# Three chained layers on one Trainium2 core: the first feed-forward gets half products and sums in DRAM, and one planner orders the whole program

## Chip, core and metric

The kernel runs on one core of a Trainium2 chip. The metric is device microseconds of one execution. TensorE (PE in the rows) multiplies matrices, VectorE (DVE) and ScalarE (ACT) work elementwise, GpSimd (POOL) and SyncE (SP) here mainly issue transfers.

## The reference

Linear attention without softmax, an RMS norm per head, then two feed-forwards over 2304 tokens of 512 features:

```python
kv  = einsum('bhsd,bhse->bhde', k, v)        # 4 batches, 8 heads, 576 tokens, head size 64
out = einsum('bhsd,bhde->bhse', q, kv)
x   = out / sqrt(mean(out**2, -1) + 1e-6) * g_norm          # then (2304, 512)
xn  = x / sqrt(mean(x**2, -1) + 1e-6) * rms_g
x   = (silu(xn @ w_gate) * (xn @ w_val)) @ w_out            # d_ff = 1536
h   = x @ w_in2
y   = where(h > 0, h, exp(min(h, 0)) - 1) @ w_out2          # d_ff = 2048
```

The weights come as 64-bit floats.

## The kernel before

**Tiling.** Features stand on partitions, tokens in columns. The 18 token tiles form five blocks: block 0 of 256 columns, blocks 1 to 4 of 512. A slice f is 128 columns of d_ff: 12 in the first feed-forward (phase 0), 16 in the second (phase 1). Every product in float32 is made of three matmuls on halves: high x high, high x low, low x high (lines 364 to 366). ScalarE rounds to the high half, VectorE subtracts to get the low one (`ah` and `al`, `xh` and `xl`). The four chunks of 128 features are c = 0 to 3.

**Weights.** `load` brings a tile of 512 KB on SP's queue into a staging buffer (`st`, `sx`: four). `convert` turns the 64-bit floats into a float32 and its halves in nine steps, seven on VectorE, one on ScalarE, one more on VectorE (lines 324 to 357).

**Phase 0.** For each f and block: gate product `pg`, value product `pv` (4 chunks x 3 matmuls each), `silu` on ScalarE, product on VectorE, halves, and then four output chunks `pb`. f = 0 and 1 stand alone (`LONE`), while attention still runs; from f = 2 on two f make a group whose output products share a bank. VectorE adds each into `acc` on chip (line 422). After the last group it is split into the new x.

**Phase 1.** Two f form a group. For the pairs of blocks (1, 2) and (3, 4), `hidden_pair` makes the four products of two f and two blocks from seven half products (Winograd's form of Strassen's scheme): sums of weights S1 to S4, sums of x T1 to T4, and ScalarE copies of partial results (`u`). Pair (3, 4) is still plain in the first two groups. Output chunks go through a buffer `part` to DRAM: the first group is written (SP), the others are added by accumulating transfers that GpSimd issues (line 618), and the last one is fetched back and added (`sofar`, line 610).

**Order.** The first stage (attention, f = 0 and 1, weights up to f = 3) is laid out by the class `Plan`: every step has an engine, a length in us, a rank and what it comes after, and the step that can start first is emitted next. What follows is written in order, with the framework's own scheduler.

Of the kernel before, what the change touches and what calls it, by code (L numbers as in the profile page):

```python
# [21 lines left out]
INF_FIELD = 2.0**-96 * 1.875  # L22


class Plan:
# [4 lines left out]
    LAG = {"DVE": (0.11, 0.13), "ACT": (0.15, 0.17), "POOL": (0.05, 0.1), "PE": (0.0, 0.15), "DMA": (0.0, 0.1)}  # L30

    def __init__(self):
        self.steps, self.ends, self.clock, self.lasts = {}, {}, {}, {}

    def add(self, name, engine, length, rank, call, after, tag=None):
        self.steps[name] = dict(
            engine=engine, length=length, rank=rank, call=call, after=list(after), tag=tag
        )
        self.clock.setdefault(engine, 0.0)

    def frees(self, tag, taker, users):

        self.lasts[tag, taker] = users

    def start(self, name, taken, bufs):
        s = self.steps[name]
        at = self.clock[s["engine"]]
        after = list(s["after"])
        if s["tag"] and len(taken[s["tag"]]) >= bufs[s["tag"]]:
            after += self.lasts.get((s["tag"], taken[s["tag"]][-bufs[s["tag"]]]), [None])  # L50
        for x in after:
            if x not in self.ends:
                return None
            engine = self.steps[x]["engine"]
            at = max(at, self.ends[x] + self.LAG[engine][engine != s["engine"]])
        return at

    def run(self, bufs):
        taken = {tag: [] for tag in bufs}
        left = {}  # L60
        for name, s in self.steps.items():
            left.setdefault(s["engine"], []).append(name)
        while any(left.values()):
            best = None
            for names in left.values():
                for name in names:
                    at = self.start(name, taken, bufs)
                    if at is not None:
                        key = at, self.steps[name]["rank"]
                        if best is None or key < best[0]:  # L70
                            best = key, name
            if best is None:
                raise ValueError(f"no step can start: {[n[:4] for n in left.values()]}")
            (at, _), name = best
            s = self.steps[name]
            left[s["engine"]].remove(name)
            if s["tag"]:
                taken[s["tag"]].append(name)
            self.clock[s["engine"]] = self.ends[name] = at + s["length"]
            s["call"]()  # L80
# [3 lines left out]
def linear_attention__swiglu__elu_kernel(  # L84
# [11 lines left out]
    out0: bass.AP,  # L96
    seq: int,
# [6 lines left out]
    F1, F2 = w_gate.shape[0], w_in2.shape[0]  # L104

# [7 lines left out]
    NMAX = 4 * P  # L113
    block_of = {i: (t, i - a) for t, (a, n) in enumerate(blocks) for i in range(a, a + n)}

# [3 lines left out]
    wp = ctx.enter_context(tc.tile_pool(name="wp", bufs=1))  # L119
    st = ctx.enter_context(tc.tile_pool(name="st", bufs=2))  # L120
    ap = ctx.enter_context(tc.tile_pool(name="ap", bufs=3))
    tp = ctx.enter_context(tc.tile_pool(name="tp", bufs=3))
    sp = ctx.enter_context(tc.tile_pool(name="sp", bufs=4))
    banks = ctx.enter_context(ExitStack())
    ps = banks.enter_context(tc.tile_pool(name="ps", bufs=1, space=PSUM))

    PSUM_BUFS = {"g": 3, "o": 5}

    def psum(tag, name):
        return ps.tile([P, 512], F32, tag=tag, name=name, bufs=PSUM_BUFS[tag])  # L130

    staged = ["st", "sx"]

    def stage(src, name):
        staged.append(staged.pop(0))
        t = st.tile([P, 2 * DM], src.dtype, tag=staged[-1], name=name)
        nc.sync.dma_start(out=t, in_=src)
        return t


    blank = const.tile([P, P], F32, name="blank")
    nc.vector.memset(blank, 0.0)
    idle = psum("g", "idle")
# [9 lines left out]
    junk = const.tile([P, DM + 1], mybir.dt.bfloat16, name="junk")  # L153

    Z = 6
    z_sb = [res.tile([P, DM + 1], F32, tag=f"z{j}", name=f"z{j}") for j in range(Z)]
# [7 lines left out]
    kv_blocks = [res.tile([P, KD, P], F32, tag=f"kvb{j}", name=f"kv{j}") for j in range(2)]  # L164
# [19 lines left out]

    def load_kv_tile(i):
        in_sb[i] = home(i)
        nc.sync.dma_start(out=in_sb[i], in_=kv[i].rearrange("t j e -> t (j e)"))
# [6 lines left out]
    def sum_kv(b, i):  # L194

        tiles = tiles_of_batch(b)
        if i == tiles[0]:
            kv_acc[b] = psum("g", f"kv{b}").rearrange("p (a e) -> p a e", a=KD)
# [17 lines left out]
    def load_q(j):  # L216
        src = q[j].rearrange("d j a t -> d (j a t)")
        if f"q{j}" in homes:
            q_sb[j] = home(f"q{j}")
            nc.sync.dma_start(out=q_sb[j], in_=src)  # L220
        else:
            q_sb[j] = stage(src, f"q{j}")
# [60 lines left out]
    def new_x(t):  # L283
        n = blocks[t][1] * P
        xh[t] = res.tile([P, KD, n], F32R, tag=f"xh{t}", name=f"xh{t}")
        xl[t] = res.tile([P, KD, n], F32R, tag=f"xl{t}", name=f"xl{t}")

    def turn(p, half):

        pt = pt_t[p, half] = psum("o", f"pt{p}_{half}").rearrange("p (c n) -> p c n", c=2)  # L290
# [18 lines left out]
    raw_sb, ready = {}, {}  # L309

    def load(src, kind, name, bufs):
        raw_sb[name] = stage(src.bitcast(U32), "r" + name)

    def convert(src, kind, name, bufs):
# [3 lines left out]
        def begin():  # L318
            raw = raw_sb.pop(name).rearrange("p (n w) -> p n w", w=2)
            t["low"], t["high"] = raw[:, :, 0], raw[:, :, 1]  # L320
            t["c"] = tp.tile([P, DM], U32, tag="tA", name="c" + name)


            nc.vector.tensor_scalar(t["c"], t["high"], 0x7FFFFFFF, None, op0=ALU.bitwise_and)
# [8 lines left out]
        def sign():  # L333
            t["w"] = tp.tile([P, DM], U32, tag="tB", name="w" + name)
# [12 lines left out]
        def add():  # L347
            wf = t["w"].bitcast(F32)
            nc.vector.tensor_tensor(wf, wf, t["c"].bitcast(F32), op=ALU.add)

        def part():
            t["h"] = wp.tile([P, DM], F32R, tag="h" + kind, name="h" + name, bufs=bufs)
            nc.scalar.activation(t["h"], t["w"].bitcast(F32), AF.Copy)

        def rest():
            l = wp.tile([P, DM], F32R, tag="l" + kind, name="l" + name, bufs=bufs)
            nc.vector.tensor_tensor(l, t["w"].bitcast(F32), t["h"].bitcast(F32), op=ALU.subtract)
            ready[name] = t["h"], l

        return [begin, scale, shift, sign, field, low, add, part, rest]  # L360

    def product(acc, w, s, xs, first, last):
        (wh, wl), (mh, ml) = w, xs
        nc.tensor.matmul(acc, wh[:, s], mh, start=first, stop=False)  # L364
        nc.tensor.matmul(acc, wh[:, s], ml, start=False, stop=False)  # L365
        nc.tensor.matmul(acc, wl[:, s], mh, start=False, stop=last)  # L366

    def into(acc, w, t):
        for c in range(KD):
            product(acc, w, slice(c * P, (c + 1) * P), (xh[t][:, c, :], xl[t][:, c, :]), c == 0, c == KD - 1)  # L370

    def act_tiles(n, name):
        h = ap.tile([P, NMAX], F32R, tag="ah", name="ah" + name, bufs=5)
        l = ap.tile([P, NMAX], F32R, tag="al", name="al" + name, bufs=5)
        return h[:, :n], l[:, :n]

    def split_act(a, n, name):
        h, l = act_tiles(n, name)
        nc.scalar.activation(h, a, AF.Copy)  # L379
        nc.vector.tensor_tensor(l, a, h.bitcast(F32), op=ALU.subtract)  # L380
        return h, l

    def gate(pg, n, name):
        s = tp.tile([P, NMAX], F32, tag="tA", name="s" + name)[:, :n]
        nc.scalar.activation(s, pg, AF.Silu)  # L385
        return s

    def gated(s, pv, n, name):
        a = tp.tile([P, NMAX], F32, tag="tB", name="a" + name)[:, :n]
        nc.vector.tensor_tensor(a, s, pv, op=ALU.mult)  # L390
        return a

    def hidden1(w, t, name):
        n = blocks[t][1] * P
        wg, wv = w
        pg = psum("g", "pg" + name)[:, :n]
        into(pg, wg, t)
        pv = psum("g", "pv" + name)[:, :n]
        into(pv, wv, t)
        return split_act(gated(gate(pg, n, name), pv, n, name), n, name)  # L400
# [581 lines left out]
```

## Time and profile before

| | |
|---|---|
| median of 3 runs | 890.13 us (889.74 to 890.29) |
| span of the profiled execution | 889.4 us |
| TensorE busy | 876.3 us |
| VectorE busy | 644.0 us |
| ScalarE busy | 409.6 us |
| GpSimd busy | 139.3 us |

The profile is of one execution; its span is the time from the first to the last instruction, and the median of the runs is 0.7 us longer. Busy times are unions of what an engine's instructions took. An engine can be busy and still be late: only where the last engine of a chain waits does it cost time.

### The profile page before, as it was taken

The page shows a single profiled execution, that of the slowest core. Times are in us where ns is not written, and L with a number is a line of the kernel's source. Part 1 is how long each engine was busy: PE and PEld are TensorE (multiplying, and loading weights), DVE is VectorE, ACT ScalarE, POOL GpSimd, SP SyncE. Part 2 cuts the span into 40 slices and gives each one's busy share as a digit, 9 for nine tenths or more (in the row PEclk, how much of TensorE's full clock was granted, in tenths as well). Part 3 has the DMA queues.
Part 4 walks back from the last instruction along what each step waited for, and adds up shares of the span by engine and source line. Part 5 has one row for each costly group of instructions (what it writes and reads, how often), then busy time and mean ns, then how long its engine had stood idle before and what let it go on. Part 6 is the DMA issues. An engine that isn't in the chain of part 4 may idle for free.

```text
span 889.4 us, 11683 instructions
## 1 busy us (share of the span) xinstructions
PE 876.3 (99%) x4324; PEld 738.8 (83%) x4324; DVE 644.0 (72%) x1229; ACT 409.6 (46%) x787; POOL 139.3 (16%) x160
## 2 busy tenths in 40 slices
PE   8999999999999999999999999999999999999998
PEld 7988888888888888888888888788888888888786
DVE  6798996567648467656867698796868677776655
ACT  2778532211212212121233577576767676666651
POOL 2465000000000000000000000033342424241400
PEclk9999999999999999999999999999999999999999
DMA  9732220102102002010200014588685949394964
GB/s 365 299 119 72 71 73 24 48 24 71 41 31 72 24 24 69 27 47 25 74 22 24 1 48 166 142 171 137 131 177 109 198 89 205 78 200 66 254 202 166
DMA packets 37145, 93.07 MB, mean 105 GB/s; under 512 B 4192, under 2 KB 4192, under 8 KB 37088
## 3 DMA queue, kind: packets, MB, share of 16 engines
q1 hardware_dynamic: 21536, 64.01, 20.4%
q0 software_dynamic: 15552, 28.32, 19.0%
q8 instruction: 34, 0.56, 0.2%
q14 instruction: 23, 0.19, 0.1%
HBM read 54.56 MB, written 37.75 MB: 104 GB/s over the span
## 4 chain that ended last, share of the span: by engine, by line
PE 69%; issue 13%; POOL 7%; DMA 5%; DVE 3%; ACT 2%; SPq 0%; POOLq 0%; ACTq 0%
PE pb L365 9%; PE pb L364 8%; PE pb L366 8%; POOL out L618 6%; PE pg L364 5%; PE pg L365 5%; PE pg L366 5%; PE pv L364 5%; PE pv L365 5%; PE pv L366 5%; PE pa L544 3%; DMA out<-part 3%; PE pc L544 2%; PE ph L364 1%; PE ph L366 1%
## 5 line engine op out<-in xcount | busy, mean ns | idle before, releaser
L618 POOL DMA_DIRECT2D out<-part x108 | 95.7, 950 | 651.7 <-ACT part L614 648.7
L379 ACT ACTIVATE ah<-a 128x512 fp32r<-128x512 f32 (+1 forms) x130 | 76.4, 590 | 157.0 <-DVE a L390 130.0
L390 DVE TENSOR_TENSOR a<-s,pv 128x512 f32<-128x512 f32 (+1 forms) x60 | 37.9, 633 | 105.4 <-PE pv L366 105.4
L380 DVE TENSOR_TENSOR al<-a,ah 128x512 fp32r<-128x512 f32 (+1 forms) x130 | 82.2, 634 | 37.7 <-ACT ah L379 37.6
L365 PE MATMUL pb<-al,hp 128*128 128x512 f32 x256 | 100.3, 392 | 0.0
L366 PE MATMUL pb<-ah,lp 128*128 128x512 f32 x256 | 99.7, 389 | 0.0
L614 ACT ACTIVATE part<-pb 128x512 f32<-128x512 f32 x126 | 73.6, 597 | 44.3 <-PE pb L366 23.3
L364 PE MATMUL pb<-ah,hp 128*128 128x512 f32 x256 | 93.0, 391 | 0.9 <-ACT part L614 0.5
L364 PE MATMUL pb<-ah,ho 128*128 128x512 f32 (+1 forms) x240 | 88.9, 370 | 0.8 <-DVE xl L304 0.4
L365 PE MATMUL pb<-al,ho 128*128 128x512 f32 (+1 forms) x240 | 88.7, 370 | 0.6 <-DVE al L784 0.6
L364 PE MATMUL pg<-xh,hg 128*128 128x512 f32 (+1 forms) x240 | 89.0, 371 | 0.0
L365 PE MATMUL pg<-xl,hg 128*128 128x512 f32 (+1 forms) x240 | 88.4, 368 | 0.0
L364 PE MATMUL pv<-xh,hv 128*128 128x512 f32 (+1 forms) x240 | 88.4, 368 | 0.0
L366 PE MATMUL pg<-xh,lg 128*128 128x512 f32 (+1 forms) x240 | 88.3, 368 | 0.0
L365 PE MATMUL pv<-xl,hv 128*128 128x512 f32 (+1 forms) x240 | 88.3, 368 | 0.0
L366 PE MATMUL pb<-ah,lo 128*128 128x512 f32 (+1 forms) x240 | 88.3, 368 | 0.0
L366 PE MATMUL pv<-xh,lv 128*128 128x512 f32 (+1 forms) x240 | 88.3, 368 | 0.0
L422 DVE TENSOR_TENSOR acc<-acc,pb 128x512 f32<-128x512 f32 (+1 forms) x120 | 74.1, 629 | 7.0 <-PE pb L366 6.3
L385 ACT ACTIVATE s<-pg 128x512 f32<-128x512 f32 (+1 forms) x60 | 33.3, 555 | 81.4 <-PE pg L366 77.9
L365 PEld LDWEIGHTS pb<-al,hp 128*128 128x128 f32 x256 | 48.1, 188 | 11.4 <-DVE al L380 1.7
L364 PEld LDWEIGHTS pb<-ah,hp 128*128 128x128 f32 x256 | 47.7, 188 | 11.7 <-ACT part L614 0.9
L366 PEld LDWEIGHTS pb<-ah,lp 128*128 128x128 f32 x256 | 48.1, 188 | 9.9
(187 smaller groups left out, 1879.2 us busy)
## 6 DMA issues: line engine op xcount, KB each, us to landing
out<-part POOLq DMA_DIRECT2D x108, 256.0 KB, 6.9
ri<-in_w_in SPq DMA_DIRECT2D x16, 512.0 KB, 4.0
rp<-in_w_out SPq DMA_DIRECT2D x16, 512.0 KB, 5.8
rg<-in_w_gate SPq DMA_DIRECT2D x12, 512.0 KB, 3.2
rv<-in_w_val SPq DMA_DIRECT2D x12, 512.0 KB, 3.2
ro<-in_w_out SPq DMA_DIRECT2D x12, 512.0 KB, 3.6
out<-part SPq DMA_DIRECT2D x18, 256.0 KB, 2.1
out<-sofar SPq DMA_DIRECT2D x18, 256.0 KB, 2.0
```

Source lines behind the costliest of these rows:

```text
L364: nc.tensor.matmul(acc, wh[:, s], mh, start=first, stop=False)
L365: nc.tensor.matmul(acc, wh[:, s], ml, start=False, stop=False)
L366: nc.tensor.matmul(acc, wl[:, s], mh, start=False, stop=last)
L379: nc.scalar.activation(h, a, AF.Copy)
L380: nc.vector.tensor_tensor(l, a, h.bitcast(F32), op=ALU.subtract)
L385: nc.scalar.activation(s, pg, AF.Silu)
L390: nc.vector.tensor_tensor(a, s, pv, op=ALU.mult)
L422: nc.vector.tensor_tensor(acc_t[t][:, e, :], acc_t[t][:, e, :], po, op=ALU.add)
L544: nc.tensor.matmul(acc, l[:, sl], r, start=first and c == 0 and i == 0, stop=c == 1 and i == 2, skip_group_check=True,)
L614: nc.scalar.activation(part, po, AF.Copy)
L618: nc.gpsimd.dma_start(out=dst, in_=part, accum_op=ALU.add)
```

## The change

All of the program is now steps of one `Plan`, phase 1 too. The planner got slots: a step `takes` a place of a kind (a bank, a half of a weight, a scratch tile), and a place is free when its last users have ended. A step has a latency `lat` behind its length, used for transfers: a load counts 5.5 us after its issue, an accumulating transfer 6.0. From f = 2 on two staging buffers remain; the other two hold T2 of pair (1, 2).

In phase 0, gate and value of one f play the part that two f play in phase 1: pair (1, 2) goes by seven half products from f = 2, pair (3, 4) from f = 4 (`PAIRED_FROM`). In phase 1 both pairs do so in every group. The sums of phase 0 leave the chip: each output chunk goes through `part` to a DRAM tensor `mid`, written for f = 0 and accumulated for the rest, and the last group's is fetched (`far`) and added on VectorE, then split and combined into the sums of x.

In a weight's conversion, masking and multiplying give way to one `tensor_scalar`, and the addition is an integer one; halves are taken of twice the value with a factor 0.5.

```diff
+PAIRED_FROM = (2, 4)
...
-        def field():
-            nc.vector.tensor_scalar(t["c"], t["w"], 0xFF800000, None, op0=ALU.bitwise_and)
-        def low():
-            cf = t["c"].bitcast(F32)
-            nc.vector.scalar_tensor_tensor(cf, t["low"], 2.0**-52, cf, op0=ALU.mult, op1=ALU.mult)
+        def tail():
+            nc.vector.tensor_scalar(t["c"], t["low"], 2.0**52, 2.0**-29, op0=ALU.add, op1=ALU.mult)
         def add():
-            wf = t["w"].bitcast(F32)
-            nc.vector.tensor_tensor(wf, wf, t["c"].bitcast(F32), op=ALU.add)
+            nc.vector.tensor_tensor(t["w"], t["w"], t["c"], op=ALU.add)
...
+    PRODUCTS = [(1, "a", 11, 11, True), (2, "b", 12, 21, True), (6, "a", 2, 2, False), (7, "c", 3, 3, True),
+                (5, "a", 1, 1, False), (3, "a", 4, 22, False), (4, "c", 22, 4, False)]
...
-                nc.vector.tensor_tensor(acc_t[t][:, e, :], acc_t[t][:, e, :], po, op=ALU.add)
+                def dump(e=e, key=key):
+                    x = live[key] = place(key)[:, :n]
+                    nc.scalar.activation(x, pbank["b", k, t, e][:, :n], AF.Copy)
+                def write(e=e, key=key):
+                    nc.sync.dma_start(out=where(ph, t, e), in_=live.pop(key))
+                def accumulate(e=e, key=key):
+                    nc.gpsimd.dma_start(out=where(ph, t, e), in_=live.pop(key), accum_op=ALU.add)
...
+            def fetch(e=e, fkey=fkey):
+                x = fetched[ph, t, e] = place(fkey)[:, :n]
+                nc.sync.dma_start(out=x, in_=where(ph, t, e))
+            def finish(e=e):
+                x = fetched[ph, t, e]
+                nc.vector.tensor_tensor(x, x, pbank["b", k, t, e][:, :n], op=ALU.add)
...
+            def silu(j):
+                nc.scalar.activation(u(j), u(j), AF.Silu)
+            def gate2():
+                live[skey] = place(skey)
+                nc.scalar.activation(live[skey], pbank[unit, "a"], AF.Silu)
```

How the order moves, at three places. First TensorE in phase 0, at block 1 of f = 4 before, and at the pair (1, 2) of f = 5 now (`pu, 0, 5, 1` is the unit's bank, `Sh` and `Sl` are halves of a sum of weights, `T` is a sum of x, `b_2_0` an output chunk of block 2):

```order
L364 MATMUL pg_4_1_2152<-xh_487,hg_1673 128x512
L365 MATMUL pg_4_1_2152<-xl_488,hg_1673 128x512
L366 MATMUL pg_4_1_2152<-xh_487,lg_1675 128x512
L364 MATMUL pg_4_1_2152<-xh_487,hg_1673 128x512
L365 MATMUL pg_4_1_2152<-xl_488,hg_1673 128x512
```

```order
L529 MATMUL ('pu', 0, 5, 1)_a<-xh_640,Sh_g_0_2271 128x512
L529 MATMUL ('pu', 0, 5, 1)_a<-xl_641,Sh_g_0_2271 128x512
L529 MATMUL ('pu', 0, 5, 1)_a<-xh_640,Sl_g_0_2281 128x512
...
L529 MATMUL ('pu', 0, 5, 1)_c<-T_1_877,h_v_2162 128x512 x2
L529 MATMUL ('pu', 0, 5, 1)_c<-T_1_877,l_v_2170 128x512
...
L719 MATMUL hid_g_5_0_2533<-xh_338,h_g_2097 128x256
```

Where 12 matmuls stood for one kind and one block, six stand for a half product of two chunks, and narrow products of block 0 fill in between.

Second VectorE between the phases: before at block 1 of the last group (`acc`, `xl` of the new x, `wi` and `li` a weight of phase 1), now at blocks 1 and 2 (`far` is a fetched sum):

```order
L422 TENSOR_TENSOR acc_1_711<-acc_1_711,pb_10_1_1_4017 128x512
L449 TENSOR_TENSOR xl_4014<-acc_1_711,xh_4013 128x512
L349 TENSOR_TENSOR wi_4053<-wi_4053,ci_4049 128x512
L422 TENSOR_TENSOR acc_1_711<-acc_1_711,pb_10_1_2_4027 128x512
L449 TENSOR_TENSOR xl_4014<-acc_1_711,xh_4013 128x512
```

```order
L693 TENSOR_TENSOR far_1_0_4347<-far_1_0_4347,b_1_0_4533 128x512
L405 TENSOR_SCALAR c_i_4553<-raw_i_4450 128x512
L409 TENSOR_SCALAR c_i_4553<-c_i_4553 128x512
L693 TENSOR_TENSOR far_1_2_4352<-far_1_2_4352,b_1_2_4545 128x512
L1148 TENSOR_TENSOR xl_4491<-far_1_0_4347,xh_4490 128x512
L693 TENSOR_TENSOR far_2_0_4359<-far_2_0_4359,b_2_0_4527 128x512
L1148 TENSOR_TENSOR xl_4491<-far_1_2_4352,xh_4490 128x512
L832 TENSOR_TENSOR far_1_0_4347<-far_2_0_4359,far_1_0_4347 128x512
L693 TENSOR_TENSOR far_2_2_4365<-far_2_2_4365,b_2_2_4561 128x512
L693 TENSOR_TENSOR far_1_1_4371<-far_1_1_4371,b_1_1_4572 128x512
L839 TENSOR_TENSOR T_1_4494<-far_1_0_4347,T_1_4494 128x512
```

The sums of x for the pair now follow the last additions directly, on the same engine, with ScalarE's roundings between them.

Third SP's queue in the first stage, from the loads of q on (`q` is a load, `raw` and `rg` a weight's, `mid<-part` a write of a sum):

```order
L137 DMA ro_580<-in_w_out 128x1024
L137 DMA q_599<-in_q 128x1024
L137 DMA q_612<-in_q 128x1024
L137 DMA q_673<-in_q 128x1024
L137 DMA rg_804<-in_w_gate 128x1024
```

```order
L242 DMA raw_o_500<-in_w_out 128x1024
L660 DMA mid<-part_0_0_550 128x256
L660 DMA mid<-part_0_1_558 128x256
L660 DMA mid<-part_0_2_579 128x256
L660 DMA mid<-part_0_3_583 128x256
L242 DMA q_619<-in_q 128x1024
L242 DMA q_670<-in_q 128x1024
L660 DMA mid<-part_1_0_688 128x512
L660 DMA mid<-part_1_1_696 128x512
L660 DMA mid<-part_1_2_716 128x512
L242 DMA q_734<-in_q 128x1024
```

Writes that wait for ScalarE's dumps now stand ahead of the last three loads of q.

## Rows read from the trace of the kernel before

**Rows 1.** The page, parts 1 and 2 (TensorE's busy tenths by slice).

```profile
span 889.4 us, 11683 instructions
PE 876.3 (99%) x4324; PEld 738.8 (83%) x4324; DVE 644.0 (72%) x1229; ACT 409.6 (46%) x787; POOL 139.3 (16%) x160
...
PE   8999999999999999999999999999999999999998
```

**Rows 2.** Busy time by stage; columns: stretch, length, engines, clock, DMA.

```profile
0.00:45.00 45.00, 40.25 (x306) 38.32 (x307) 33.02 (x68) 22.00 (x50) 16.19 (x28) 0.96 0.83 328
45.00:113.00 68.00, 66.96 (x387) 57.42 (x388) 62.22 (x133) 48.22 (x108) 27.38 (x24) 1.00 0.25 86
113.00:500.00 387.00, 387.00 (x1866) 327.14 (x1865) 257.12 (x480) 89.56 (x155) 0.00 (x0) 1.00 0.12 41
500.00:595.00 95.00, 93.35 (x453) 78.37 (x452) 81.15 (x157) 63.74 (x121) 8.93 (x10) 1.00 0.39 110
595.00:835.00 240.00, 239.42 (x1094) 197.27 (x1093) 180.48 (x347) 163.24 (x313) 82.21 (x93) 1.00 0.75 147
835.00:890.00 55.00, 49.33 (x226) 40.27 (x225) 29.99 (x49) 22.86 (x43) 4.59 (x6) 0.98 0.65 195
```

**Rows 3.** Timeline of TensorE: wide matmuls around 240, narrow around 126.6.

```profile
239.66 0.39 PE L366 MATMUL pb<-ah,lo 128*128 128x512 f32 x1
...
251.90 0.39 PE L366 MATMUL pg<-xh,lg 128*128 128x512 f32 x1
...
126.58 0.28 PE L364 MATMUL pg<-xh,hg 128*128 128x256 f32 x1
126.70 0.28 PE L365 MATMUL pg<-xl,hg 128*128 128x256 f32 x1
```

**Rows 4.** What TensorE waited for: us in total, times, longest.

```profile
PE ph L364 <- DVE u L555: 1.6, 2, 0.8
...
PE ph L364 <- DVE acc L422: 0.9, 1, 0.9
...
PE pb L365 <- DVE al L784: 0.6, 2, 0.4
```

**Rows 5.** Timeline of VectorE around 100 us: starts of back-to-back instructions.

```profile
99.53 0.68 DVE L422 TENSOR_TENSOR acc<-acc,pb 128x512 f32<-128x512 f32 x1
100.13 0.42 DVE L324 TENSOR_SCALAR cg<-rg 128x512 uint32<-128x512 uint32 x1
100.47 0.42 DVE L324 TENSOR_SCALAR cv<-rv 128x512 uint32<-128x512 uint32 x1
```

**Rows 6.** Timeline of ScalarE around 700 us.

```profile
699.47 0.58 ACT L614 ACTIVATE part<-pb 128x512 f32<-128x512 f32 x1
699.95 0.62 ACT L411 ACTIVATE e<-e 128x512 f32<-128x512 f32 x1
700.47 0.62 ACT L523 ACTIVATE Sh_i<-S_i 128x512 fp32r<-128x512 f32 x1
```

**Rows 7.** Line 618, the accumulating transfers: issue in ns, landing in us.

```profile
L618 POOL DMA_DIRECT2D out<-part x108: 856/865/1540, 569.8 to 843.9; - x108
...
DMA to landing us min/median/max: 4.0/6.9/10.0
```

**Rows 8.** Timeline of TensorE at 112 us.

```profile
112.40 0.50 PE L365 MATMUL pb<-al,ho 128*128 128x512 f32 x1 [0.23 <-DVE al L784]
```

**Rows 9.** DMA issues: KB each, median us to landing.

```profile
out<-sofar SPq DMA_DIRECT2D x18, 256.0 KB, 2.0
...
q<-in_q SPq DMA_DIRECT2D x6, 512.0 KB, 5.1
...
sofar<-out SPq DMA_DIRECT2D x10, 256.0 KB, 6.5
```

**Rows 10.** Timeline of TensorE, its last matmul.

```profile
885.00 0.39 PE L366 MATMUL pb<-hp,al 128*128 128x512 f32 x1
```

**Rows 11.** Busy time from 510 to 540 us, columns as in rows 2.

```profile
510.00:540.00 30.00, 30.00 (x149) 25.47 (x148) 28.38 (x58) 22.72 (x46) 0.00 (x0) 1.00 0.30 101
```

More of the change, by code (lines that the diff above doesn't have):

```diff
@@ L21, with __init__, add @@
 WARM = 16
-INF_FIELD = 2.0**-96 * 1.875
+INF_FIELD = 2.0**-96 * 1.75
 class Plan:
[L30 to L35, printed above, removed]
+    LAG = {"DVE": (0.09, 0.13), "ACT": (0.11, 0.17), "POOL": (0.05, 0.1), "PE": (0.0, 0.15), "DMA": (0.0, 0.1), "ADD": (0.0, 0.1), "NOTE": (0.0, 0.0)}
+    PATIENCE = 0.03
+    def __init__(self, kinds):
+        self.kinds, self.holder, self.where, self.users = kinds, {}, {}, {}
+        self.steps, self.ends, self.clock = {}, {}, {}
+        self.log = []
+    def add(self, name, engine, length, rank, call, after=(), takes=(), lat=0.0):
+        assert name not in self.steps, name
@@ L36, in add @@
         self.steps[name] = dict(
-            engine=engine, length=length, rank=rank, call=call, after=list(after), tag=tag
+            engine=engine, length=length, rank=rank, call=call, after=list(after), takes=list(takes), lat=lat
         )
         self.clock.setdefault(engine, 0.0)
[L41 to L63, printed above, removed]
-            best = None
[L65 to L71, printed above, removed]
-            if best is None:
[L73 to L80, printed above, removed]
+    def frees(self, key, users):
+        self.users[key] = list(users)
@@ new lines, in holds, with reach, room @@
+    def holds(self, slot, key, users):
+        self.holder[slot] = key
+        self.users[key] = list(users)
+    def reach(self, name, engine):
+        e = self.steps[name]["engine"]
+        return self.ends[name] + self.LAG[e][e != engine]
+    def room(self, kind, engine, chosen):
+        best = None
+        for slot in self.kinds[kind]:
+            if slot in chosen:
+                continue
+            key = self.holder.get(slot)
+            at = 0.0
+            if key is not None:
+                if any(u not in self.ends for u in self.users[key]):
+                    continue
+                at = max((self.reach(u, engine) for u in self.users[key]), default=0.0)
+            if best is None or at < best[0]:
+                best = at, slot
+        return best
@@ L163, in linear_attention__swiglu__elu_kernel @@
     kv_sb = {}
[L164 removed]
+    kv_blocks = [res.tile([P, DM], F32, tag=f"kvb{j}", name=f"kv{j}").rearrange("p (a e) -> p a e", a=KD) for j in range(2)]
     for t in kv_blocks:
@@ L183, in home, with stage @@
         return wait[tag][:, j, :]
+    def stage(src, key):
+        t = res.tile([P, 2 * DM], src.dtype, tag=plan.where[key], name="_".join(map(str, key)))
+        nc.sync.dma_start(out=t, in_=src)
+        return t
     def load_kv_tile(i):
@@ L333, in sign @@
         def sign():
-            t["w"] = tp.tile([P, DM], U32, tag="tB", name="w" + name)
+            t["w"] = place(("w", n), U32)
             nc.vector.scalar_tensor_tensor(
@@ L355, in rest @@
[L355 to L400, printed above, removed]
@@ new lines, in conversion, with load @@
+        for j, (fn, engine, length, takes) in enumerate(seq_):
+            plan.add((n, j), engine, length, rank + j * 0.1, fn, [(n, j - 1)] if j else [("in", n), *after, *chain[-1:]], takes)
+        chain.append((n, 5))
+        plan.frees(("raw", n), [(n, 4)])
+        plan.frees(("c", n), [(n, 5)])
+        plan.frees(("w", n), [(n, DONE), *(summed or ())])
+        plan.frees(("h", n), users)
+        plan.frees(("l", n), users)
+    raw_sb, chain = {}, []
+    def load(n):
+        raw_sb[n] = stage(weight[n].bitcast(U32), ("raw", n))
@@ new lines, in linear_attention__swiglu__elu_kernel, with half_product @@
+    PRODUCTS = [(1, "a", 11, 11, True), (2, "b", 12, 21, True), (6, "a", 2, 2, False), (7, "c", 3, 3, True),
+                (5, "a", 1, 1, False), (3, "a", 4, 22, False), (4, "c", 22, 4, False)]
+    pbank, live = {}, {}
+    def half_product(unit, X, one, two, m, c):
+        _, b, a, x, first = next(p for p in PRODUCTS if p[0] == m)
+        if first and c == 0:
+            pbank[unit, b] = bank((unit, b))
+        (wh, wl), at_ = A(one, two, a)
+        sl = slice(at_ + c * P, at_ + (c + 1) * P)
+        mh, ml = (y[c] for y in B(X, x))
+        for i, (l, r) in enumerate(((wh, mh), (wh, ml), (wl, mh))):
+            nc.tensor.matmul(
+                pbank[unit, b], l[:, sl], r, start=first and c == 0 and i == 0, stop=c == 1 and i == 2,
+                skip_group_check=True,
+            )
```

1095 lines of the change are left out of this document (643 added, 452 removed).

## The prediction

> **What bounds the kernel now.** I began with the page's first two parts: TensorE is busy 876.3 of 889.4 us and in almost every slice 9 tenths, while VectorE has 72% and ScalarE 46% [rows 1]. Busy shares of pipelined matmuls overlap, so I next cut the span into stages [rows 2]: from 113 to 500 us TensorE is busy 387.00 of 387.00 us at granted clock 1.00, and the missing 13.1 us lie in the first 45 us (4.75), from 45 to 113 (1.04), from 500 to 595 (1.65), from 595 to 835 (0.58) and behind 835 (5.07). Then the timeline, for what one matmul really costs: from 239.66 to 251.90 us 54 wide matmuls (512 columns) pass, 0.2267 us from start to start, though each "lasts" 0.39; narrow ones (256 columns) start 0.12 us apart [rows 3]. So the kernel is a row of matmuls at these pitches with almost no holes, and its time moves with the number of matmuls. The list of what TensorE waits for confirms it: apart from first loads, its longest entry is 1.6 us, two waits for an addition of VectorE [rows 4].
>
> **What the change removes.** A pair of 512-token blocks against the gate and value slices of one f takes 2 blocks x 2 kinds x 4 chunks x 3 = 48 wide matmuls in the plain way. Seven half products of two chunks take 7 x 2 x 3 = 42. Blocks 1 and 2 go that way from f = 2 (10 units), blocks 3 and 4 from f = 4 (8 units): 18 x 6 = 108 fewer. In the second feed-forward blocks 3 and 4 were still plain in the first two groups; now they are paired: 2 x 6 = 12 fewer. The built orders count 3276 wide matmuls before and 3156 after, 624 narrow in both. 120 x 0.2267 = **27.2 us**, wherever no new hole opens.
>
> The pitch is that of these very forms, in an unbroken stream at full clock [rows 2, 3]. The Trainium skill, page "TensorE: Matmul & The Clock Gate", section "Back-to-back issue gap", gives about 131 ns for a sustained stream with 512 columns; by that figure the saving would be 15.7 us, an estimate. No stream in this trace runs so fast, so the row decides.
>
> **What it adds, engine by engine.** VectorE's pitches are 0.60 us for two inputs of 512 and 0.34 for one [rows 5] (rows show 0.69 and 0.42 because neighbours overlap). Removed: 120 additions into the sums held on chip and one pass of 0.60 per weight tile (68 tiles). Added: 54 additions in the new units, weight sums for ten f, sums of x, 20 last additions. Every instruction of each order at its pitch gives 618 us before, 606 after. One operation the trace lacks: the step add is now an integer addition of 1024 halves. Its nearest row is the old addition of the same tile (0.60), which I take; at twice the elements it is 1.20, and 68 x 0.60 = 41 us more, still 75% of the span.
>
> ScalarE gains 172 wide instructions (20 dumps per group instead of additions, snaps, halves of sums) at 0.48 to 0.52 us [rows 6]: 373 to about 468 us at these pitches, 54% of the span. GpSimd issues 100 more accumulating DMAs at 0.87 us [rows 7]: 87 us, on an engine with 139 us busy.
>
> These engines are not the bound on the average, so I looked where they are tight.
>
> *First stage (to f = 3).* Before, TensorE waits here twice for the low half of an activation, 0.6 us in all [rows 4]; the later place is block 4, f = 0, at 112.40 us [rows 8]. Up to it VectorE's order holds 90.0 us of work and TensorE's 99.8 us: 9.8 us of lead are just too few there, since VectorE lost more to the first loads. In the new order that place has 95.6 against 105.7 (10.1); the others up to the weights of f = 3 have 11 to 16 (weights of v2 12.7, sums of g2 12.9, of g3 14.4). So I book 0. With the addition at 1.20, 6 conversions lie ahead of that place, 3.6 us, partly under waits for loads: at worst +3. The writes to DRAM stand between the loads of q on SP's queue: the first q behind four writes can be issued about 50.4 us (b_0_0_3 at 38.2 in TensorE's order, 11 us of holes, 0.48 for the dump) and lands 5.1 us later [rows 9]; tile 12 needs it at 52 + 11 = 63. Hidden by 7 us.
>
> *The sums in DRAM.* A dump slot (five of them) is held for the dump, the issue and the landing, 0.6 + 0.87 + 6.9 = 8.4 us [rows 7, 9]. Eight tiles of a pair come 1.36 us apart (6 x 0.2267), so the sixth dump waits 8.4 - 6.8 = 1.6 us, and four banks cover 4 x 1.36 = 5.4 us. The old second feed-forward has just this pattern, and there TensorE lost 0.58 us in 240 [rows 2]. I book 0 for the first.
>
> *Between the feed-forwards.* Here sums are fetched, added, split, and combined for both pairs. From the first such addition on (TensorE has ended b_6_1_0) to the last third half product of pair 3, VectorE's order holds 98 instructions: 80 of 0.60, 10 of 0.33, 8 of 0.34, 54.2 us; TensorE's holds 222 wide and 48 narrow matmuls, 56.1 us. Margin 1.9 us over all; at the other uses between, 2.0 to 2.9. Before, the transition cost 0.9 + 1.6 us of waits [rows 4], which go. New ones come if a fetch lands late: the slot for the sixth fetch is free 3.6 us of VectorE's order ahead of its addition. Nearest rows for a 256 KB transfer on SP: 2.0 us (store, quiet queue) and 6.5 us (fetch behind accumulates) [rows 9]. No accumulates run in that stretch, so nearer to 2.0, hidden; at 6.5 each of two pairs is 2.9 us late, less the margin: +4. I book 2.5, as much as the old waits: net 0.
>
> *End.* The last matmul starts at 885.00, and 4.4 us of addition, store and closing follow [rows 10]; the new order ends with the same steps.
>
> **Sum.** 889.4 - 27.2 + 0 + 0 + 0 = 862.2 us of span. The median of the runs is 890.13, 0.7 us over this span, so **862.9 us**. Bounds of the terms: +3 (first stage), +6.5 (transition, with the old waits as gain -2.5), and as gain all old holes behind the first loads and ahead of the tail, 1.0 + 1.7 + 0.6 + 1.0 = 4.3 us [rows 2, 10].
>
> **Rivals.**
> *Transition opens.* VectorE's 1.9 us margin ignores the passing of each tile between VectorE and ScalarE (add, high, low, combine, high, low). Two such chains late by 4 to 5 us each: 863 + 9 = 872. For it: 97% load over 56 us. Against: the pairs' products stand interleaved with other blocks' work, and from 510 to 540 us of the old trace VectorE is busy 28.38 of 30 us and TensorE 30.00 [rows 11].
> *First stage opens.* The q loads behind writes, or sums of x for pair 1 between normalisation steps, are late by more than their 7 us, once or twice: 868 to 874, say 870.
> *Old holes vanish too*, by the last term above: 858.6.
> *A removed matmul gives back less than its pitch*, at the least that of a narrow one [rows 3]: 120 x 0.12 = 14.4 us, 876. The unbroken stream from 113 to 500 us speaks against it. (It is the Trainium skill's figure above that would lead there.)
> *Slower than before.* A landing that lasts longer in the first feed-forward: a clump of eight dumps holds ScalarE for L + 1.5 - 6.8 us; the banks cover 5.4; what is left stops TensorE, since the snaps of the next unit are behind on ScalarE. Five groups with two clumps: 10 x (L - 10.7). This eats 27.2 us from L = 13.4 us on; at 14.5 us it is +38, 901 us. The landings before are 4.0, 6.9, 10.0 (least, median, most) [rows 7], beside a VectorE that converts weights all the while. The Trainium skill, page "SBUF — State Buffer", section "SBUF: two separate sides", warns of this mechanism: descriptors that GpSimd writes starve while VectorE holds the shared port, with about 620 ns grown to 3100 ns. By that rule, as an estimate, landings would grow by 2.5 us, to 9.4. The trace shows issues of 865 ns as median and 1540 at most, so little of it is seen here.
> That the change does not do what it says I exclude: the counts are in the built order.
>
> **Chances.** Forecast (859 to 868): 0.70. Transition 872: 0.13. First stage 870: 0.07. Old holes gone, below 859: 0.05. Removed ones worth less: 0.01. Slower: 0.04. The range is 857 to 874: it takes in the forecast, nearly all of both stall cases (up to 11 us) and most of the fourth; outside lie about 0.1 and what I can't name. No change would be within 0.2% (1.8 us), about what a measurement of this kernel can tell. All cases but the last lie at least 14 us below that: faster 0.94, same 0.02, slower 0.04.
>
> **What will show it.** Wide starts 0.2267 us apart and 3156 of them. TensorE idle under 15 us in all, with no hole above 2 us between 113 us and the end. A transition (about 449 to 505 us: 436 and 492 in TensorE's order and some 12.5 us of first holes) with VectorE above 27 of each 30 us and TensorE missing at most 3 us; if it misses more, the releaser tells which: VectorE's sums (the rival) or a DMA into far. Landings of part near 7 us and ScalarE's waits for them under 2 us each; above 13 the slower rival holds. The integer addition near 0.69 us as shown, not 1.2. What would make it wrong most likely: a wait in a chain that crosses engines, which sums per engine can't see.

## The result, and the profile after

The changed kernel takes 863.48 us (median of 4 runs, 863.01 to 864.4) against 889.93 us before: ratio 0.9703, 95% interval 0.969 to 0.9717. The forecast was 862.9 us, range 857 to 874. The profiled execution took 863.61 us, its span is 861.6; the sum of the forecast gave 862.2 for the span.

The page of the changed kernel: span, its first part (busy time, share, instructions), and of the second TensorE and its granted clock.

```profile
span 861.6 us, 12089 instructions
PE 849.0 (99%) x4204; PEld 713.8 (83%) x4204; DVE 641.4 (74%) x1217; ACT 511.0 (59%) x979; POOL 232.8 (27%) x260
...
PE   7999999999999999999999999999999999999998
...
PEclk9999999999999999999999999999999999999999
```

TensorE has 120 matmuls fewer (4324 before, [rows 1]) and is as full as before. ScalarE and GpSimd rose by 101 and 94 us of busy time; waits for ScalarE cost TensorE 0.5 us in all, and none is for GpSimd behind the first loads. Busy time by stage (columns as in [rows 2]), in the stages as they lie now, and further below pieces for the experiments:

```profile
0.00:45.00 45.00, 40.23 (x325) 37.93 (x326) 33.04 (x68) 23.12 (x52) 19.51 (x30) 1.00 0.89 351
45.00:113.00 68.00, 65.84 (x372) 56.02 (x373) 63.57 (x129) 52.81 (x118) 33.74 (x28) 1.00 0.39 109
113.00:449.00 336.00, 335.92 (x1630) 282.64 (x1630) 251.39 (x477) 169.46 (x314) 83.94 (x94) 1.00 0.63 127
449.00:505.00 56.00, 54.70 (x258) 44.38 (x256) 52.27 (x95) 33.89 (x62) 0.00 (x0) 1.00 0.28 85
505.00:835.00 330.00, 329.70 (x1522) 274.60 (x1522) 227.76 (x431) 227.19 (x428) 95.63 (x108) 1.00 0.76 151
835.00:862.00 27.00, 22.57 (x103) 18.22 (x102) 13.37 (x21) 4.50 (x9) 0.00 (x0) 0.99 0.63 215
...
120.00:150.00 30.00, 29.96 (x144) 24.90 (x143) 27.13 (x51) 19.70 (x36) 8.80 (x10) 1.00 0.90 191
150.00:180.00 30.00, 30.00 (x156) 25.63 (x155) 28.80 (x60) 14.04 (x27) 4.74 (x5) 1.00 0.47 106
...
450.00:515.00 65.00, 63.40 (x295) 50.97 (x294) 60.75 (x112) 41.19 (x75) 0.00 (x0) 1.00 0.33 105
515.00:600.00 85.00, 85.00 (x398) 71.21 (x397) 73.55 (x143) 63.63 (x121) 18.04 (x21) 1.00 0.66 150
600.00:835.00 235.00, 235.00 (x1086) 195.95 (x1085) 144.78 (x271) 156.05 (x294) 77.59 (x88) 1.00 0.80 149
```

Read second minus third number as TensorE's idle time: 4.77, 2.16, 0.08, 1.30, 0.30, and 4.03 in the last stage (the span ends at 861.6), 12.6 us in all where it was 13.1. So 889.4 - 27.2 (120 x 0.2267) - 0.5 = 861.7, and 861.6 was measured. The pitch can be read in the chain that ended last (start, us, what):

```profile
547.83 13.60 PE b L622 x60
```

13.60 / 60 = 0.2267 us, as before.

The two spans have to be compared with care. Every execution whose span is on record lasts 1.7 to 2.1 us longer than that span, so the execution profiled before, with its 889.4 us, lasted about 891.2 us, an estimate, some 1.1 us more than the median of 890.13. Its trace has a place where it lost about as much. After a wait for a load, 16 matmuls take 3.60 us (start, us, what); the granted clock of TensorE in the 5 us around them is 0.66 (columns as in [rows 2], TensorE alone):

```profile
20.52 3.60 PE L202 MATMUL kv<-wacc 128*128 128x128 f32 x16 [1.76 <-DMA wacc<-in_kv]
```

```profile
20.00:25.00 5.00, 4.49 (x26) 0.66 1.03 410
```

In the changed kernel that wait is 0.90 us, and 8 such matmuls behind it take 1.16 us at a granted clock of 1.00. So the spans fell by 27.8 us and the medians by 26.5; the medians say what the change is worth, 0.6 to 0.7 us less than the term of 27.2.

What TensorE waited for (total, times, longest), first loads left out:

```profile
PE b L622 <- DVE z L321: 1.5, 1, 1.5
...
PE b L622 <- DVE far L693: 0.7, 1, 0.7
PE b L622 <- DVE xl L363: 0.5, 2, 0.3
PE ('pu', 1, 0, 1)_a L529 <- ACT ('pu', 1, 0, 1)_u L551: 0.3, 1, 0.3
```

The waits of 1.6 (two of them) and 0.9 us of [rows 4] are gone; the longest new one is at 99.5 us: a bank of PSUM that the output products want is still held by an attention tile until VectorE has scaled it (L321). The integer addition (line, engine, operation, names, shape, count, busy us and mean ns), and then the dumped sums of the first feed-forward (issue min/median/max in ns, landing in us):

```profile
L425 DVE CUSTOM_DVE_ANT_0 w_p<-w_p,c_p 128x1024 uint16<-128x1024 uint16 x16 | 11.0, 688 | 0.3
```

```profile
L663 POOL DMA_DIRECT2D mid<-part x100: 858/875/2097, 95.5 to 421.6; - x100
...
DMA to landing us min/median/max: 3.2/5.7/10.3
```

And the list of DMA issues (KB each, median us to landing), where [rows 9] stood:

```profile
out<-part POOLq DMA_DIRECT2D x108, 256.0 KB, 5.4
mid<-part POOLq DMA_DIRECT2D x80, 256.0 KB, 6.3
...
far<-mid SPq DMA_DIRECT2D x16, 256.0 KB, 2.7
```

(The 5.7 us above is the median of all 100, with the 20 smaller ones of block 0; 6.3 is that of the 80 of 256 KB.) ScalarE's waits for a landing, in all, times and longest, first in the second feed-forward, then in the first:

```profile
ACT part L657 <- DMA out<-part: 17.1, 11, 3.5
...
ACT part L657 <- DMA mid<-part: 3.6, 3, 1.6
```

### The profile page after: what moved, and what is told of

The parts are those of the page before. It is cut to its first block, busy times and chain, and to the rows that moved or that the text cites. A ratio compares the mean times of both kernels' runs of the same rounds, so it can differ in the third digit from the quotient of the medians.

```text
span 861.6 us, 12089 instructions
## 1 busy us (share of the span) xinstructions
PE 849.0 (99%) x4204; PEld 713.8 (83%) x4204; DVE 641.4 (74%) x1217; ACT 511.0 (59%) x979; POOL 232.8 (27%) x260
## 4 chain that ended last, share of the span: by engine, by line
PE 85%; DVE 7%; DMA 3%; ACT 2%; issue 1%; POOL 1%; SPq 0%; ACTq 0%; POOLq 0%; DVEq 0%
PE b L622 36%; PE hid_v L719 4%; PE hid_g L719 4%; PE hid_i L719 2%; PE po L298 1%; PE kv L262 1%; DMA wacc<-in_kv 1%; DMA wxl<-in_kv 1%; DVE xl L363 1%; POOL ri L318 1%; DVE far L693 1%; DVE act L584 1%; PE ('pu', 0, 9, 1)_a L529 1%; PE ('pu', 0, 11, 1)_a L529 1%; PE ('pu', 0, 4, 1)_a L529 1%
## 5 line engine op out<-in xcount | busy, mean ns | idle before, releaser
L657 ACT ACTIVATE part<-b 128x512 f32<-128x512 f32 (+1 forms) x246 | 138.8, 574 | 85.1 <-PE b L622 61.6
L622 PE MATMUL b<-act,h_p 128*128 128x512 f32 x512 | 158.5, 390 | 0.3 <-DVE act L584 0.2
L663 POOL DMA_DIRECT2D mid<-part x100 | 89.8, 995 | 234.7 <-ACT part L657 227.1
L622 PE MATMUL b<-act,h_o 128*128 128x512 f32 (+1 forms) x480 | 137.6, 370 | 3.0 <-DVE z L321 1.5
L622 PEld LDWEIGHTS b<-act,h_p 128*128 128x128 f32 x512 | 95.3, 188 | 21.1 <-DVE act L584 0.5
L622 PEld LDWEIGHTS b<-act,h_o 128*128 128x128 f32 x480 | 87.1, 188 | 21.7 <-DVE z L321 2.0
L622 PE MATMUL b<-act,l_p 128*128 128x512 f32 x256 | 99.6, 389 | 0.0
L622 PE MATMUL b<-act,l_o 128*128 128x512 f32 (+1 forms) x240 | 88.3, 368 | 0.0
L622 PEld LDWEIGHTS b<-act,l_p 128*128 128x128 f32 x256 | 48.1, 188 | 10.0
L584 DVE TENSOR_TENSOR act<-e,act 128x512 fp32r<-128x512 f32 (+1 forms) x80 | 49.6, 631 | 1.5 <-ACT act L580 1.2
```

The costliest lines, as they stand in the source:

```text
L584: nc.vector.tensor_tensor(l, src(), h.bitcast(F32), op=ALU.subtract)
L622: nc.tensor.matmul(po, l, r, start=f == fs[0] and i == 0, stop=f == fs[-1] and i == 2)
L657: nc.scalar.activation(x, pbank["b", k, t, e][:, :n], AF.Copy)
L663: nc.gpsimd.dma_start(out=where(ph, t, e), in_=live.pop(key), accum_op=ALU.add)
```

## The experiments

Theory: the gain is the number of wide matmuls times their pitch, and all the rest of the change is hidden. Rivals: the plan or the sums in DRAM give or take something of their own; the transition between the feed-forwards or the landings of dumps are near to opening. All ratios are to the kernel before.

### e1, e2: the half products of the first feed-forward taken back

```diff
-PAIRED_FROM = (2, 4)
+PAIRED_FROM = (12, 12)   # e1: none; the rooms of the sums of x are then taken at the second feed-forward
+PAIRED_FROM = (8, 8)     # e2: 8 units instead of 18
```

> No half products in the first feed-forward; plan, sums in DRAM, conversion and second feed-forward stay as after the change. 108 wide matmuls come back (3264). By the prediction's first term (a wide matmul is worth its pitch, 0.2267 us, all else is hidden): 863.5 + 24.5 = 888.0 us, within 2. If a removed matmul is worth only a narrow one (0.12): 876.4. If the plan or the sums in DRAM give something of their own, the time stays under 886; if they cost something that the half products hide, it is above 890.

> Half products of the first feed-forward from f = 8 on for both pairs of blocks: 8 units instead of 18, 60 wide matmuls more than after the change (3216). Pitch theory: 863.5 + 13.6 = 877.1 us, within 1.5, on the straight line between the changed kernel and the one without half products there. At 0.12 each: 870.7. If the first stage is relieved by the later sums of x (the holes of about 3 us from 90 to 120 us close), 874 to 876.

e2: 877.24 us (ratio 0.9857, 0.9842 to 0.9872): 13.76 us for 60 matmuls, 0.229 each. e1: 890.78 us (1.0007, 0.9998 to 1.0017; 889.13 to 892.03): 27.3 us for 108, 2.8 more than expected. That is outside the 2 us that I allowed, in the range (above 890) of the rival that the plan or the sums in DRAM cost something that the half products hide. With 12 wide matmuls fewer than the kernel before, e1 takes as long as it (890.21 in the same rounds): without the half products of the first feed-forward the rest of the change gains nothing. At 0.12 us for a matmul both runs would lie far lower, so that rival is out. Where a part of e1's rest is, its windows show:

```profile
450.00:515.00 65.00, 64.47 (x311) 53.93 (x310) 53.38 (x95) 30.94 (x55) 0.00 (x0) 1.00 0.23 68
515.00:600.00 85.00, 81.48 (x372) 67.36 (x371) 63.91 (x120) 58.92 (x111) 8.73 (x10) 0.98 0.50 137
```

TensorE misses 4.05 us from 450 to 600 us, where the changed kernel misses 1.60; one wait of 3.5 us for VectorE's low half of an activation. So the plan finds another order there, a worse one; from 45 to 113 us it is a better one (0.41 us missing instead of 2.16). The profiled execution of e1 took 889.13 us; the 1.65 us from there to the median of its ten no row shows.

### e3: half products earlier

```diff
-PAIRED_FROM = (2, 4)
+PAIRED_FROM = (2, 2)
```

> Both pairs from f = 2: two units more, 12 wide matmuls fewer (3144). Count alone: 863.5 - 2.7 = 860.8 us. Theory of the balance: VectorE is busy 112 of the 120 us from 45 to 165 us, and about 20 us of it (sums of x for blocks 3 and 4, two units' sums) come there earlier; what does not fit into the 8 us free and cannot be put off stops TensorE. Then 866 to 872, say 868, with TensorE waiting for VectorE between 90 and 200 us.

864.72 us (0.9717, 0.9702 to 0.9731; the changed kernel has 863.48): 1.2 us slower with 12 matmuls fewer, so 4 us of new holes. Direction and place are the theory's; the size is half of it, and the time lies below its range. First two stretches, then TensorE's new waits there:

```profile
120.00:150.00 30.00, 28.00 (x134) 22.96 (x133) 28.70 (x56) 18.60 (x36) 9.28 (x11) 1.00 0.86 174
150.00:180.00 30.00, 28.36 (x145) 23.40 (x144) 28.04 (x56) 14.95 (x29) 3.40 (x5) 1.00 0.40 92
```

```profile
PE hid_v L719 <- ACT s L785: 1.5, 1, 1.5
...
PE b L622 <- ACT part L657: 1.4, 1, 1.4
...
PE ('pu', 0, 2, 3)_b L529 <- DVE sa L739: 0.6, 1, 0.6
```

TensorE misses 3.64 us in 60 where the changed kernel misses 0.04. Two of the three waits lead to VectorE, as the theory said: the last one directly, the first by a silu for which ScalarE had waited 2.99 us for VectorE. The middle one does not: that dump had waited 1.38 us for a landing into `mid`. So fewer matmuls are not always faster here.

### e4, e5, e6: the latencies that the plan counts

```diff
 # e4: no load has a latency
-    DONE, LOAD = 7, 5.5
+    DONE, LOAD = 7, 0.0
...
-        plan.add(("in", x), "NOTE", 0.0, k, None, [("go", x)], lat=0.1 + late)
+        plan.add(("in", x), "NOTE", 0.0, k, None, [("go", x)], lat=0.1)
 # e5 (0.0) and e6 (2.0): only the fetches of sums
-            plan.add(("fetch", ph, t, e), "NOTE", 0.0, 0, None, [("look", ph, t, e)], lat=LOAD)
+            plan.add(("fetch", ph, t, e), "NOTE", 0.0, 0, None, [("look", ph, t, e)], lat=0.0)
```

> The plan counts every load as landed as soon as its transfer time of 1.27 us is over (latency 0 instead of 2.0 or 5.5 us); all else as after the change, so VectorE's order puts conversions ahead of data. Theory: VectorE waits for raw tiles (median 4 to 7 us to landing) up to 4 us at each of some dozen weights where it is over 90% busy (45 to 210 us) and at the transition; 868 to 880, say 872. Rival: two staging buffers are filled so early that the order hardly changes anything: 862 to 865.5.

> The plan counts only the fetches of sums (into far) as landed after their transfer time; weights keep their latency. It splits the 31 us that the run without any latency lost. Theory (the forecast's rival on the transition): VectorE's additions into far come about 2 us ahead of the landing (2.7 us), in both pairs, and each wait is passed on; TensorE misses 8 to 15 us instead of 3.2 between 450 and 510 us: 868 to 876, say 871. If the weights' latency did all of it: 862 to 865.

> The fetches of sums counted with 2.0 us instead of 5.5, near to what the traces show (2.1 to 2.7 to landing, of which the plan has 0.64 as transfer). Theory: the latency in the plan is safe but too long, additions can start 3.5 us earlier and part of the 3.2 us that TensorE misses between 450 and 510 us goes: 861.5 to 863. Rival: the order gets too tight for the fetches that land late, 864 to 868.

e4: 894.13 us (1.0031, 1.0014 to 1.0048), 31 us over the changed kernel: the whole gain is gone, far beyond the 880 that I allowed. e5: 880.68 us (0.9896, 0.9882 to 0.9911), 17.2 over, beyond the 876 that I allowed. e6: 868.65 us (0.9766, 0.9748 to 0.9785), 5.2 over: my theory fell, its rival held. First e4, then e5:

```profile
450.00:515.00 65.00, 52.96 (x227) 41.98 (x226) 55.42 (x99) 35.62 (x62) 0.00 (x0) 0.89 0.23 69
515.00:600.00 85.00, 85.00 (x391) 70.74 (x390) 59.08 (x114) 57.42 (x106) 14.23 (x16) 1.00 0.65 154
600.00:835.00 235.00, 224.64 (x1017) 185.66 (x1016) 151.67 (x286) 151.96 (x288) 76.53 (x84) 0.98 0.78 137
```

```profile
505.00:510.00 5.00, 0.00 (x0) 0.75 0.20 52
...
sum 65.00, PE 52.94; mean PE 10.59
```

From 450 to 515 us the two kernels lose the same (52.96 and 52.94 of 65 us), so there it is the fetches. Of the some 15 us that this stretch costs e5 (229 matmuls start in it instead of 295, at 0.2267 us for a wide one) 10.5 are more idle time; the rest is the clock (0.89 in both). What e4 loses behind 600 us (10.4 us idle, and a clock of 0.98) is not in e5. VectorE waits there four times for raw tiles, 17.1 us in all (2.0 in the changed kernel), so it most likely belongs to the weights; a run with their latency alone is missing. In e5 VectorE waits six times for far, 5.2 us in all; TensorE then stands 6.4 us for one sum of a pair's unit. e6's hole is of another kind. TensorE around it:

```profile
495.14 0.39 PE L529 MATMUL ('pu', 1, 0, 1)_c<-T,l_i 128*128 128x512 f32 x1
500.81 0.79 PE L529 MATMUL ('pu', 1, 0, 3)_a<-xh,h_i 128*128 128x512 f32 x1 [5.28 <-DVE ('pu', 1, 0, 1)_u L555]
501.40 0.63 PE L529 MATMUL ('pu', 1, 0, 3)_a<-xl,h_i 128*128 128x512 f32 x1
501.83 0.63 PE L529 MATMUL ('pu', 1, 0, 3)_a<-xh,l_i 128*128 128x512 f32 x1
...
504.84 0.42 PE L529 MATMUL ('pu', 1, 0, 3)_b<-xh,l_i 128*128 128x512 f32 x1
505.09 0.40 PE L529 MATMUL ('pu', 1, 0, 3)_b<-xh,h_i 128*128 128x512 f32 x1
```

TensorE stands 5.28 us for a sum of VectorE, but VectorE waits only 0.8 us for transfers there: it is busy 54.77 of 56 us, with other additions ahead of that one. A shorter latency gave not a late datum but another order, in a stretch without room for one. What made the plan choose it is open. (The execution traced here took 870.93 us, the median of e6 is 868.65.)

### e7: more work for VectorE in the transition

```diff
-                nc.vector.tensor_tensor(xl[t][:, e, :], fetched[0, t, e], xh[t][:, e, :].bitcast(F32), op=ALU.subtract)
+                for _ in range(2 if t else 1):
+                    nc.vector.tensor_tensor(xl[t][:, e, :], fetched[0, t, e], xh[t][:, e, :].bitcast(F32), op=ALU.subtract)
...
-            plan.add(("nl", t, e), "DVE", dve(n), rank + 0.1 * e, low, [("nh", t, e)])
+            plan.add(("nl", t, e), "DVE", dve(n) * 2 if t else dve(n), rank + 0.1 * e, low, [("nh", t, e)])
```

> In the transition the low half of each new activation of blocks 1 to 4 is computed twice (12 more VectorE instructions of 0.60 us, 7.2 us, counted in the plan; the result is the same). Forecast's margin (54.2 us of VectorE against 56.1 of TensorE): 7.2 - 1.9 = 5.3 us more, 868.8 us, holes between 450 and 515 us. If VectorE's work there can be put off behind the stretch: under 865. If each chain over ScalarE adds to it: over 872.

872.35 us (0.9804, 0.9785 to 0.9823): 8.9 us for 7.2 us of work, more than the margin's account and just in the range of "each chain adds to it". But the traces speak against that reading: TensorE is idle for 15.9 us of the span where the changed kernel has 12.6, only 3.3 more, less than the 5.3 of the margin's account. The other 5.6 us are busy time for the same 4204 matmuls (849.0 us in the changed kernel), and a lower granted clock stands beside them. First the page's line, then two stretches:

```profile
PE 854.6 (98%) x4204; PEld 716.3 (82%) x4204; DVE 649.5 (75%) x1229; ACT 511.1 (59%) x979; POOL 232.9 (27%) x260
```


```profile
475.00:480.00 5.00, 2.93 (x7) 0.70 0.20 59
480.00:485.00 5.00, 4.66 (x14) 0.62 0.42 124
```

From 480 to 485 us TensorE is busy 4.66 us and starts 14 matmuls, where 22 wide ones pass at full clock. A margin of 1.9 us did not take up 7.2 us of work, and the holes cost more than their length.

### e8: three tiles for dumped sums

```diff
-        "A": AD, "A1": ["y0", "t3"], "P": P3 + K2, "U": Z4 + ["t2"], "C": ["t0", "t1", "t2"],
+        "A": AD, "A1": ["y0", "t3"], "P": P3, "U": Z4 + ["t2"], "C": ["t0", "t1", "t2"],
```

> Three tiles for dumped sums instead of five (the plan knows). A slot is held for dump, issue and landing, 0.6 + 0.9 + 5.4 to 6.3 us, so dumps can pass one per 2.3 to 2.6 us on the mean, where a clump of eight tiles comes 1.36 us apart. Theory of the forecast's slower rival (what the banks don't cover stops TensorE, 3 us for each clump, some 24 of them): 880 to 910, say 890, with ScalarE waiting for landings. Rival: the plan spreads the groups, so that only few clumps are left: 863 to 868.

907.28 us (1.0196, 1.0181 to 1.0211), but not where my slower rival had it:

```profile
113.00:449.00 336.00, 336.00 (x1632) 282.19 (x1631) 251.74 (x477) 165.71 (x312) 83.82 (x94) 1.00 0.67 127
449.00:505.00 56.00, 51.24 (x242) 41.26 (x241) 53.65 (x97) 33.70 (x62) 0.00 (x0) 1.00 0.29 90
505.00:835.00 330.00, 311.30 (x1384) 251.66 (x1383) 217.71 (x408) 205.62 (x388) 79.15 (x90) 0.98 0.68 123
```

The first feed-forward, whose sums the change moved to DRAM, loses nothing with three tiles. The second, which had its sums there before, loses 18.7 us of TensorE by 835 us: its groups come faster (18 tiles in some 41 us against 20 in some 67), and ScalarE waits there 17 times for a landing, 24.0 us in all. That the landings cause the loss is argued, not shown: the plan made another order for three tiles. Over the whole span TensorE is idle 30.0 us longer than in the changed kernel and busy 14.6 us longer with the same matmuls.

### e10: additions of the transition on GpSimd

```diff
-                plan.add(name, "DVE", EW, r, lambda x=b[x], y=b[y], z=b[into]: less(x(), y(), z()), done[x] + done[y] + done[into])
+                on, engine, length = (nc.gpsimd, "POOL", 1.1) if ph and j == 4 else (nc.vector, "DVE", EW)
+                plan.add(name, engine, length, r, lambda x=b[x], y=b[y], z=b[into], on=on: less(x(), y(), z(), on), done[x] + done[y] + done[into])
```

(and so for its low half)

> In the transition the fourth sum of x of each pair and its low half (8 instructions of 512, 4.8 us of VectorE) go to GpSimd, which has nothing to do there (0.00 us busy from 449 to 505 us); the plan counts 1.1 us for each, a guess. Theory: what TensorE still misses there (3.2 us) comes from VectorE's load of 97%, so 1 to 2.5 us go: 861 to 862.5. Rival: the same work on GpSimd lasts much longer than 1.1 us or slows VectorE's instructions beside it, and the last products wait: 864 to 872.

866.79 us (0.9742, 0.9729 to 0.9755), 3.3 slower: the rival. Groups of GpSimd's instructions:

```profile
L832 POOL TENSOR_TENSOR far<-far,far 128x512 f32<-128x512 f32 x4 | 11.0, 2760 | 72.7 <-DVE far L832 47.6 <-ACT act L580 16.3 <-ACT xh L835 8.8
L839 POOL TENSOR_TENSOR T<-far,T 128x512 fp32r<-128x512 f32 x4 | 5.4, 1342 | 6.5 <-ACT T L835 6.5
```

A subtraction that takes VectorE 0.68 us takes 2.76 on the mean here (1.34 into the low half), so the fourth sum comes later than the plan counts (1.1 us). VectorE's instructions beside it lengthened as well: of its low halves of the other sums, 0.68 us as median, one took 1.61 and one 1.19 us. The Trainium skill, page "GPSIMD Engine Reference", introduction, has VectorE about twice as fast in ordinary elementwise work; the trace agrees for the low halves (1.34 us against 0.68), and the subtractions were slower still.

### e12: most accumulating transfers left out

```diff
                 def accumulate(e=e, key=key):
-                    nc.gpsimd.dma_start(out=where(ph, t, e), in_=live.pop(key), accum_op=ALU.add)
+                    x = live.pop(key)
+                    if ph or k == last_k(0) - 1:
+                        nc.gpsimd.dma_start(out=where(ph, t, e), in_=x, accum_op=ALU.add)
```

> Same order of every engine, but 80 of the 100 accumulating DMAs of the first feed-forward are left out (the dumps stay, the sums miss those parts): what the way over DRAM costs where it is hidden by the forecast. Forecast's zero: 862.5 to 864.5. If issues or landings hold TensorE, or the transfers slow other loads: 858 to 862.

862.78 us (0.9698, 0.9685 to 0.9712), span 861.4 against 861.6. TensorE's busy time is the same with and without them (335.96 and 335.92 of 336 us):

```profile
113.00:449.00 336.00, 335.96 (x1633) 283.40 (x1632) 251.61 (x479) 169.33 (x314) 17.91 (x20) 1.00 0.28 73
```

GpSimd drops from 83.94 to 17.91 us and the DMA share from 0.63 to 0.28, and nothing moves. In the order of the changed kernel the way over DRAM is hidden; in that of e3 a landing cost 1.4 us.

### e9 and e11: two repeats

Two further runs were to have changed one latency each, but the edit was not in the kernels: e9 ran the same kernel as e4, e11 the changed kernel itself. What was expected of them has no run, and stands here only as the record:

> The other half of the split: only weights are counted without latency, fetches keep 5.5 us. If the two add up: 894.1 - 880.7 = 13.4 us over the changed kernel, 877, with the holes behind 600 us, where VectorE waits for raw tiles of the second feed-forward. If the weights did harm only because the transition had broken before them: 863 to 866.

> Fetches of sums counted with 8.0 us instead of 5.5 (0 gave 880.7, 2.0 gave 868.6). If safety against late fetches is all that the latency gives, 5.5 had none to gain any more: 863 to 864.5. If an order with later additions is worse by what it puts off: 865 to 868. If it goes on as from 0 to 5.5: 860 to 862.

As repeats: e11 863.75 us (0.9707, 0.9694 to 0.9721), 0.3 from the first measurement; e9 890.61 us (1.0019, 1.0003 to 1.0035), 3.5 below e4. With holes of several us in it that kernel scatters more (889.22 to 895.61) than one without, so the 31 us of e4 are 27 to 31. Not tried are therefore the weights' latency alone and a fetch latency above 5.5.

No version that computes the whole result beat the changed kernel.

## Why the prediction was right, point by point

- *The first term*, 120 x 0.2267 = 27.2 us: right; the medians fell by 26.5. e2 confirms the pitch with 0.229 us a matmul. The 15.7 us that the Trainium skill's 131 ns gave (page "TensorE: Matmul & The Clock Gate", section "Back-to-back issue gap") are refuted for this stream by the same runs.
- *First stage, booked 0*: wrong by a little. From 45 to 113 us TensorE's idle time rose from 1.04 to 2.16 us, and by a wait that my list of places lacked: not an operand but a PSUM bank held by an attention tile. My margins of VectorE's work against TensorE's at each operand can't see that. The loads of q behind writes, which I had feared, made TensorE wait nowhere (the terms of that place, 38.2 + 11 + 0.48, add up to 49.7 and not to 50.4, which changes nothing).
- *Integer addition at 0.60*: right, 0.69 us as shown where 0.68 is shown for an addition of 512 too [rows 5]. VectorE's work as a whole was to fall by 12 us (618 to 606) and its busy time fell by 2.6; why is open, and the sum holds no term of it.
- *Sums in DRAM, booked 0*: right, and e12 shows it apart. Landings 5.7 us as median, ScalarE's waits for those into mid 3.6 us in all, the longest 1.6. My sign for all of `part`, under 2 us each, failed in the second feed-forward, where the longest is 3.5 us (1.7 before); TensorE misses only 0.30 us from 505 to 835 us all the same. My price for the slower rival was too high: it took clumps of eight dumps 1.36 us apart for granted, and e8 shows that the first feed-forward's dumps pass through three tiles.
- *Transition, net 0*: right in size. 1.30 us are missing from 449 to 505, none of it a late fetch (2.7 us to landing, near to the 2.0 that I took). VectorE's load, 52.27 of 56 us, is below the 97% of the orders' count but as tight as said: e5, e6, e7 and e10 each opened it, at 3 to 17 us, a part of which is the clock behind the holes, for which I had no price. The rival of 872 was one change of order away: e6 lies at 868.65, e5 beyond it.
- *What I gave no price at all*: that loads are counted with their latency. e4 shows that without it the changed kernel would be no faster than before. The term of 27.2 us holds only "wherever no new hole opens", and this part of the change is one of the things that keep the holes shut.
- *End*: 4.03 us instead of 5.07; the hole ahead of the tail closed, which stood in the bound of gains. That it cancels the loss of the first stage is luck: neither was forecast.
- *Median and span*, booked 0.7 us: measured 1.9. The 0.7 set the median of some executions against the span of another one that lasted about 1.1 us longer, and the span from which the sum starts was too long by the same amount. The two errors cancel, so the forecast is the median of before less 27.2. It missed by 0.6 us. No row shows where these went: between the two profiled executions idle time fell by 0.5 us.

## What to carry to other kernels

In a kernel that is one unbroken row of matmuls, as this one, a removed matmul is worth its pitch in that stream, and the work that replaces it is free as long as each other engine keeps a lead at every place, not on the average. Where an engine is over 90% busy beside TensorE, a few us more of work, or only another order, cost more than their length: e7's holes grew by 3.3 us and its busy time by 5.6. A planner that orders by times must know when data lands: here the latency of fetches and weights in its account was worth as much as the whole change.

## What the runs showed of the hardware

- A hole can cost more than its length. After 5.28 us without a matmul (e6) the granted clock was 0.50 from 501 to 504 us, which is 1.2 GHz, and wide matmuls came mostly 0.43 us apart; the eight steps from 500.81 to 504.84 took 4.03 us instead of 1.81, so the hole cost 7.5 us. After the 1.53 us without a matmul before 101.37 us in the changed kernel the clock stayed at 1.00.

```profile
501.00:504.00 3.00, 2.92 (x7) 1.81 (x8) 3.00 (x6) 2.84 (x6) 0.00 (x0) 0.50 0.00 0
```

- The same subtraction of 128x512 took 0.68 us on VectorE and 1.5 to 5.1 us on GpSimd beside it, and single instructions of VectorE took up to 1.6 us meanwhile (e10).
- An integer addition of 1024 halves takes no longer (0.69 us) than an addition of 512 floats.
- 100 accumulating transfers more did not lengthen the landings: 6.3 and 5.4 us as medians for 256 KB in the two feed-forwards, 6.9 before [rows 7]; single issues of GpSimd went up to 2.1 us.
